# A gated attention and FFN kernel: the high rows of each product follow TensorE's own count, output weights are split in mid-attention, and the last stage has another order

## The chip, the cores and the metric

The kernel runs on one core of one Trainium2 chip. The metric is the device time of one execution in microseconds (us). Three runs of the kernel before gave a median of 1321.56 us (1321.49 to 1323.14). Lower is better.

## The reference

The input x has S = 2048 rows of D = 512. There are H = 32 heads of 16 that share one key and one value head, and an FFN of width F = 1792.

```python
q = (x @ wq).reshape(B, S, H, Dh).transpose(0, 2, 1, 3)
k, v = x @ wk, x @ wv                        # one head for all 32
p = softmax(einsum("bhqd,bkd->bhqk", q, k) * Dh ** -0.5)
a = einsum("bhqk,bkd->bhqd", p, v).transpose(0, 2, 1, 3).reshape(B, S, H * Dh) @ wo
b = (silu(x @ w_gate) * (x @ w_up)) @ w_down
g = sigmoid((x * gate_w).sum(-1, keepdims=True))
out = g * a + (1 - g) * b                    # all f32
```

## The kernel before

**Arithmetic.** Each f32 operand of a large product is split into a rounded high part and the rest (`xh` and `xl`, `wgh` and `wgl`, `hh` and `hl`), and a product is three matmuls: high by high, low by high, high by low. An FFN job of 128 x 512 outputs and 512 inputs so takes 12 matmuls of 128 rows; a job of the down product takes 15 or 12, for 5 or 4 blocks of F.

**Stages.** A prologue transposes x, projects keys and values (`project_kv`) and queries (`query`); in it DVE splits the key and value weights (`prepare_kv`, eight instructions, L111 and L112) between two splits of transposed x (L645 on ACT, L646 on DVE). Then comes attention with the FFN fed into it: a first part of 16 iterations, and 90 blocks of 5, 5 and 6 units (`block`, L838). A unit is one head by 128 keys: two scores (`score`, L774, into the two banks `pss`), two exponentials (ACT L785, some halves after a copy by DVE L780), and four `mix` matmuls (L801, into the bank `po`). Strings in `STEPS` and `TURN` set the order in a block, where S is a score pair and F a step of the FFN; all the block's mix matmuls follow. The block after the first part (block 0) uses `TURN[5]`, with 16 F to 10 S. At the end of a head its output is divided by the sums and stored to `o_d` in DRAM (the items in `LATER`, L812 to L817).

**F steps.** `Halves.step` (L475) cuts a job in its input rows 0 to 63 (the low lane) and 64 to 127 (the high lane), and issues one 64-row matmul for each lane that has a job; the two run side by side in the array. A job runs all its low rows, waits, and then runs its high rows into the same of three banks `pf`. The high rows may start `LAG` = 8 ticks of a step counter after the low rows end, and a bank is taken as free `SLACK` = 8 ticks after the high rows end. For the dependence between lanes, DVE writes one element (`sign`, L498) after the last low matmul, and the first high matmul waits for DVE. A lane without a job leaves its half of the step empty (`idle`). One job, number 54, has only its low rows here (`SPLIT`): its high rows were made earlier (`early`).

**Last stage.** Jobs still in `JOBS` run as 128-row matmuls (`whole`). Ahead of them SP issues loads of the last down weights (`td`, 8), then the four blocks of `wo` (`load_wo`, L142), which go through the two buffers `wraw` and are split by POOL (L152, L154), then the stores of the last head's output (L817) and the read of it (`load_o`, L527, split by POOL in L529 and L532). Then `finish` (L534) multiplies by `wo` for the four chunks of 512 rows in the order `OUTS` = 2, 3, 1, 0, adds the FFN's part and stores. The reads for the second chunk of `OUTS` are issued after all left-over jobs, those of the third and fourth after `finish` of the first and second. `acc_again` and `store_acc` (L418, L426) bring parts of the FFN's sums back and away; one core issues all these transfers on SP in the order of the program.

Of the kernel before, what the change touches and what calls it, by code (L numbers as in the profile page):

```python
# [21 lines left out]
H = 32  # L22
# [44 lines left out]
def tile_gated_mix(ctx, tc, x, wq, wk, wv, wo, w_gate, w_up, w_down, gate_w, out):  # L67
# [13 lines left out]
    x_d = dpool.tile([2, 2, P, KD, CH], F32, name="x_d")  # L81
    w_d = dpool.tile([3, NF, 2, P, D], F32, name="w_d")
    wq_v = wq.rearrange("(k p) n -> p k n", p=P)

# [7 lines left out]
    kmax = cpool.tile([P, 1], F32, name="kmax")  # L92
    sign = cpool.tile([1, 1], F32, name="sign")
    top = cpool.tile([P, KD * NCH + 1], F32, name="top")
# [44 lines left out]
    def load_split(view, name, bufs, pool=wp, order=lambda w, heads=True: w):  # L139
        shape = list(view.shape)  # L140
        raw = wp.tile(shape, F32, name="wraw", bufs=WRB)
        nc.sync.dma_start(raw, view)  # L142
        hi = pool.tile(shape, F32R, name=name + "h", bufs=bufs)
        lo = pool.tile(shape, F32R, name=name + "l", bufs=bufs)
        if pool is qpool:
            split(order(hi, False), order(lo, False), order(raw), nc.gpsimd, nc.gpsimd)
            return hi, lo
        parts = KD if pool is wp else 2
        views = [w if len(shape) == 2 else w.rearrange("p k f -> p (k f)") for w in (hi, lo, raw)]
        cuts = [slice(i * D // parts, (i + 1) * D // parts) for i in range(parts)]  # L150
        for w in cuts if pool is wp else [slice(None)]:
# [39 lines left out]
    class Job:  # L191
        def __init__(self, size, ready, terms, end):
            self.size, self.ready, self.terms, self.end, self.after = size, ready, terms, end, []
            self.only = None


        def step(self, i, half=None):
            alone = half is not None and half == self.only
            opens, closes = alone or not half, alone or half != 0
            if i == 0 and opens:  # L200
                self.ps = ps_f.tile([P, CH], F32, name="pf")
                self.terms = self.terms()
# [5 lines left out]
            ins = nc.tensor.matmul(self.ps, a, b, start=(i == 0 and opens), stop=(last and closes))  # L208
# [86 lines left out]
    def gate_up(n, c):  # L295
# [42 lines left out]
        def up(ps):  # L338
            hh = wp.tile([P, CH], F32R, name="hh", bufs=7)
            hl = wp.tile([P, CH], F32R, name="hl", bufs=7)  # L340
            if len(t) > 2:
# [7 lines left out]
            def cast():  # L349
                if n < NCH * NF - 1:  # L350
# [12 lines left out]
        if n == SPLIT:  # L363
            r[0].only = 0
        return r

# [61 lines left out]
    def jobs():  # L428
        late = []
        for m, c in enumerate(ORDER):  # L430
            for fs in GROUPS:
# [4 lines left out]
                if fs[-1] == NF - 1:  # L436
                    if m < 2:
                        new[-1].after.append(lambda m=m: load_x_again(ORDER[m + 2]))
                    elif m == NCH - 1:
                        new[-1].after.append(acc_again)  # L440
# [6 lines left out]
            late[-1].after.append(lambda c=c: store_acc(c))  # L447
        yield from late
# [19 lines left out]
    class Halves:  # L468
# [6 lines left out]
        def step(self, more):  # L475
# [14 lines left out]
            if self.low:  # L490
# [5 lines left out]
                elif not self.low:  # L496
                    self.wait.append((job, self.clock))
                    tick = nc.vector.memset(sign, 0.0)  # L498
                    follow(tick, job.lows)
                    job.lows = tick  # L500
            if self.high:
# [14 lines left out]
    def load_wo(k, pool):  # L516
        WO.append(load_split(wo[k * P:(k + 1) * P, :], f"wo{k}", 1, pool))

    def load_o(c, ks=range(KD), pool=None):
        if c not in OT:  # L520
            OT[c] = new_x(("o", c))
        for k in ks:
            if pool is None:
                raw = wp.tile([P, CH], F32, name="wraw", bufs=WRB)
            else:
                raw = pool.tile([P, CH], F32R, name="td", bufs=8).bitcast(F32)
            nc.sync.dma_start(raw, o_d[k * P:(k + 1) * P, c * CH:(c + 1) * CH])  # L527
            if c == OUTS[0]:
# [56 lines left out]
    with tc.tile_pool(name="apool", bufs=1) as ap, tc.tile_pool(name="apool2", bufs=2) as a2:  # L585
# [19 lines left out]
        def prepare_kv():  # L605
            k, v, g = slice(0, DH), slice(DH, 2 * DH), slice(2 * DH, 2 * DH + 1)
            for r in (0, RT):
                to = [w[:, :, r:r + 3 * DH].rearrange("p k (i n) -> p k i n", i=3) for w in (wkv_h, wkv_l)]
                src = wkv_f[:, :, k].unsqueeze(2).to_broadcast([P, KD, 3, DH])
                split(to[0], to[1], src, nc.vector)  # L610
            for to, src in ((3 * DH, v), (KW - 1, g)):
                rows = slice(to, to + src.stop - src.start)
                split(wkv_h[:, :, rows], wkv_l[:, :, rows], wkv_f[:, :, src], nc.vector)

# [74 lines left out]
        with tc.manual_schedule():  # L689
# [47 lines left out]
    with tc.tile_pool(name="bpool", bufs=2) as bp:  # L737
        PT = {}

        def load_head(h):  # L740
            nc.sync.dma_start(new_qs(h).bitcast(F32), q_d[h])


        SLOT, HOME, PAST, USED, OLD = {}, {}, {}, {}, {}
# [157 lines left out]
        with tc.manual_schedule():  # L902
# [25 lines left out]
            for k, (u, n) in enumerate(SPANS):  # L928
# [10 lines left out]
                if u % NT == 0 and 0 < h < H - 1:  # L939
                    load_head(h + 1)  # L940
                if k == NB - EARLY:
                    load_o(OUTS[0], range(KD - 1))
            while halves.busy():
# [6 lines left out]
    with tc.tile_pool(name="tpool", bufs=2) as tp, tc.tile_pool(name="rpool", bufs=1, side="right") as rp, \  # L950
            tc.manual_schedule():
        for f in GROUPS[-1]:
            W["d", NCH * NF - NF + f] = [tp.tile([P, D], F32R, name="td", bufs=8) for _ in range(2)]
            for j, part in enumerate(W["d", NCH * NF - NF + f]):
                nc.sync.dma_start(part.bitcast(F32), w_d[2, f, j])
        for k in range(KD):
            load_wo(k, tp)
# [12 lines left out]
        nc.sync.dma_start(ACC[0], a_d[0])  # L970
        for m, c in enumerate(OUTS):
            finish(c, tp)
            if m == 1:

# [6 lines left out]
            if m + 2 < NCH:  # L981
                load_o(OUTS[m + 2], pool=tp)

# [80 lines left out]
```

## Time and profile before

| | |
|---|---|
| median of 3 runs | 1321.56 us (1321.49 to 1323.14) |
| the profiled execution | 1323.07 us; its span in the trace is 1321.3 us, so 1.8 us lie around it |
| busy share of the span | PE 99%, ACT 81%, DVE 59%, POOL 23% |
| clock granted to TensorE | 1.00 of full speed |
| attention blocks 0 to 89 | 129.09 to 1248.24 us |
| left-over jobs in the last stage | 1248.17 to 1271.72 us |
| `finish`, to the last result | 1271.72 to 1321.3 us |

A row of the profile gives start and duration in us, the engine, the line of the program, the operation, the operands by name, and in brackets the idle time before it and what ended that. Two matmuls of 64 rows that start within 0.03 us of each other are the two lanes of one F step.

### The profile page before, as it was taken

The numbers are of one execution on the slowest core, as the hardware profiler recorded it, in microseconds if no ns is written. First come the engines' busy times: TensorE is split into PE (matmuls) and PEld (weight loads), VectorE is DVE, ScalarE is ACT, GpSimd is POOL, SyncE is SP. The second block draws the span as 40 slices with busy tenths as digits, with TensorE's granted clock in tenths as the row PEclk, the third lists the DMA queues.
The fourth block names the chain that finished last, engine by engine and source line by source line (L and its number), as shares of the span: only waits on it lengthen the run. The fifth ranks groups of instructions, "written<-read, shape, count | busy, mean of one in ns | idle before, by whom it ended". The sixth has DMA issues, their size and how long they took to land.

```text
span 1321.3 us, 27265 instructions
## 1 busy us (share of the span) xinstructions
PE 1312.7 (99%) x10767; PEld 769.3 (58%) x10767; DVE 781.7 (59%) x1340; ACT 1075.7 (81%) x1597; POOL 298.6 (23%) x737
## 2 busy tenths in 40 slices
PE   9999999999999999999999999999999999999998
PEld 7655555555555555555555655555655555655587
DVE  4655566566566666666656666666656566566632
ACT  4587888888888888888889888888889888889611
POOL 5362342264053174254120000000000000010043
PEclk9999999999999999999999999999999999999999
DMA  8668121122134264244135252242132252142264
GB/s 287 203 195 278 28 66 37 59 70 61 44 94 164 95 222 148 91 154 160 38 131 180 83 178 69 69 128 89 40 116 95 82 181 85 53 137 88 88 231 146
DMA packets 102516, 157.36 MB, mean 119 GB/s; under 512 B 11888, under 2 KB 43376, under 8 KB 100720
## 3 DMA queue, kind: packets, MB, share of 16 engines
q1 hardware_dynamic: 100656, 155.36, 36.4%
q8 instruction: 88, 1.44, 0.5%
q10 hardware_dynamic: 1728, 0.20, 0.1%
q14 instruction: 44, 0.36, 0.1%
HBM read 99.42 MB, written 55.57 MB: 117 GB/s over the span
## 4 chain that ended last, share of the span: by engine, by line
PE 98%; ACT 1%; DMA 0%; DVE 0%; POOL 0%; SPq 0%; issue 0%; ACTq 0%; POOLq 0%
PE pf L208 39%; PE po L801 34%; PE pss L774 20%; PE pf L121 3%; PE pss L641 0%; ACT pt L785 0%; DMA td<-o_d 0%; PE po L628 0%; POOL xl L532 0%; DVE xl L646 0%; PE pss L681 0%; DVE wkv_l L112 0%; ACT xh L645 0%; SPq L527 0%; DVE wkv_h L111 0%
## 5 line engine op out<-in xcount | busy, mean ns | idle before, releaser
L785 ACT ACTIVATE pt<-pss 128x1024 f32<-128x1024 f32 (+1 forms) x1024 | 787.4, 827 | 156.0 <-PE pss L774 123.2
L780 DVE COPY pt<-pss 128x512 f32<-128x512 f32 x475 | 327.9, 691 | 372.2 <-PE pss L774 367.6
L801 PE MATMUL po<-pt,vaug 128*32 128x512 f32 x4096 | 461.4, 595 | 0.0
L774 PE MATMUL pss<-qs,ks 64*128 64x512 f32 x2048 | 417.7, 410 | 0.4 <-ACT pt L785 0.4
L774 PEld LDWEIGHTS pss<-qs,ks 64*128 64x128 f32 x2048 | 200.1, 183 | 201.8 <-ACT pt L785 102.3
L801 PEld LDWEIGHTS po<-pt,vaug 128*32 128x32 f32 x4096 | 124.8, 109 | 267.2 <-issue 261.9
L785 ACT ACTIVATE pt<-pt 128x512 f32<-128x512 f32 x475 | 265.9, 630 | 0.0
L208 PE MATMUL pf<-xh,wgh 64*128 64x512 f32 (+1 forms) x444 | 160.5, 392 | 0.0
L208 PE MATMUL pf<-xl,wgh 64*128 64x512 f32 (+1 forms) x444 | 159.4, 390 | 0.0
L208 PE MATMUL pf<-xh,wgl 64*128 64x512 f32 (+1 forms) x444 | 159.3, 391 | 0.0
L208 PE MATMUL pf<-xh,wuh 64*128 64x512 f32 (+1 forms) x440 | 154.6, 391 | 0.1
L208 PE MATMUL pf<-xh,wul 64*128 64x512 f32 (+1 forms) x440 | 153.8, 391 | 0.0
L208 PE MATMUL pf<-xl,wuh 64*128 64x512 f32 (+1 forms) x440 | 153.6, 390 | 0.0
L208 PE MATMUL pf<-wdl,hh 64*128 64x512 f32 (+1 forms) x411 | 135.8, 391 | 0.0
L208 PE MATMUL pf<-wdh,hl 64*128 64x512 f32 (+1 forms) x411 | 135.6, 391 | 0.0
L208 PE MATMUL pf<-wdh,hh 64*128 64x512 f32 (+1 forms) x411 | 135.6, 391 | 0.0
L812 DVE RECIPROCAL rsb<-rsb 128x128 f32<-128x128 f32 x128 | 116.6, 933 | 2.0 <-issue 0.4
L529 POOL CAST xh<-wraw 128x512 fp32r<-128x512 f32 x4 | 2.4, 611 | 487.5 <-DMA wraw<-o_d 487.5
L208 PEld LDWEIGHTS pf<-xh,wgh 64*128 64x128 f32 (+1 forms) x444 | 76.6, 185 | 6.7 <-issue 0.6
L208 PEld LDWEIGHTS pf<-xh,wgl 64*128 64x128 f32 (+1 forms) x444 | 76.8, 185 | 5.6
L208 PEld LDWEIGHTS pf<-xl,wgh 64*128 64x128 f32 (+1 forms) x444 | 76.9, 185 | 5.2
L208 PEld LDWEIGHTS pf<-xh,wuh 64*128 64x128 f32 (+1 forms) x440 | 74.3, 185 | 7.2 <-issue 0.7
(171 smaller groups left out, 1447.2 us busy)
## 6 DMA issues: line engine op xcount, KB each, us to landing
qs<-q_d SPq DMA_DIRECT2D x31, 512.0 KB, 4.5
q_d<-hh SPq DMA_DIRECT2D x28, 256.0 KB, 4.1
wraw<-in_B_w_gate_dram SPq DMA_DIRECT2D x28, 256.0 KB, 4.0
wraw<-in_B_w_up_dram SPq DMA_DIRECT2D x28, 256.0 KB, 3.1
wraw<-in_B_w_down_dram SPq DMA_DIRECT2D x28, 256.0 KB, 3.5
wgh<-w_d SPq DMA_DIRECT2D x28, 256.0 KB, 2.7
wgl<-w_d SPq DMA_DIRECT2D x28, 256.0 KB, 3.0
wuh<-w_d SPq DMA_DIRECT2D x28, 256.0 KB, 2.7
```

The lines of the kernel that those rows point to most:

```text
L121: nc.tensor.matmul(ps, a, b, start=(i == 0), stop=(i == n - 1))
L208: ins = nc.tensor.matmul(self.ps, a, b, start=(i == 0 and opens), stop=(last and closes))
L529: nc.gpsimd.tensor_copy(OT[c][0][:, k, :], raw)
L774: nc.tensor.matmul(ps[:, b * CH:(b + 1) * CH], ks[rows, kt * P:(kt + 1) * P], QS[h][rows, j, :], start=True, stop=True)
L780: other = nc.vector.tensor_copy(pt[:, CH:], ps[:, CH:])
L785: ins = nc.scalar.activation(pt[:, w], ps[:, w], AF.Exp, scale=SCALE)
L801: ins = nc.tensor.matmul(po[c * 2 * DH:(c + 1) * 2 * DH, :], vaug[:, kt, :], pt[:, c * CH:(c + 1) * CH], start=(kt == 0), stop=(kt == NT - 1))
L812: nc.vector.reciprocal(rsb[:, w], rsb[:, w])
```

## The change

- `LAG` goes from 8 to 3 and `SLACK` from 8 to 9. The DVE instruction `sign` is gone: a TensorE `nop` after the last low matmul carries the dependence, and in the built program the first high matmul waits for TensorE's own count.
- Block 0 has its own string with 20 F to 10 S, and DVE copies three of its ten score halves.
- In the last group of FFN jobs, all gates and ups come before the late downs. Up 54 may run only once gate 54 has its bank. Results of jobs 54 and 55 lie in the tiles `wgh`, `wgl`; the high part of 54 is made by ACT, that of 55 by DVE.
- `wo` is loaded and split in mid-attention (`keep_wo`, with gate 39, 41, 43 and 45), its parts are stored to a new DRAM buffer `o_w`, and the last stage only loads the parts.
- Two of the four pairs of last down weights are loaded before the end of attention (`load_last`).
- `load_o` is divided: `fetch_o` issues the reads, `split_o` makes the parts. The reads for the second chunk come before the left-over jobs, those for the third and fourth before `finish` of the first and second. `acc_again` and the read of `again` move behind the first `finish`, the last `store_acc` behind the third.
- `prepare_kv` goes from DVE to POOL, ahead of the split of the first query weights.

```diff
-SLACK = 8
+SLACK = 9
-LAG = 8
+LAG = 3
...
+    def keep_wo(k):
+        lo, hi = [wp.tile([P, D], F32R, name="wraw", bufs=WRB) for _ in range(2)]
+        nc.sync.dma_start(lo.bitcast(F32), wo[k * P:(k + 1) * P, :])
+        for i in range(KD):
+            w = slice(i * P, (i + 1) * P)
+            nc.gpsimd.tensor_copy(hi[:, w], lo[:, w].bitcast(F32))
+            nc.gpsimd.tensor_tensor(lo[:, w], lo[:, w].bitcast(F32), hi[:, w].bitcast(F32), ALU.subtract)
+        KEPT.extend([lambda j=j, part=part: nc.sync.dma_start(o_w[k, j], part.bitcast(F32))
+                     for j, part in enumerate((hi, lo))])
...
+            if nm == "g" and n % 2 and n // 2 - NF - 5 in range(KD):
+                keep_wo(n // 2 - NF - 5)
...
             if half is not None:
                 rows = slice(half * RT, (half + 1) * RT)
                 a, b = a[rows], b[rows]
+                if half and i == 0 and not alone:
+                    follow(nc.tensor.nop(), self.lows)
             ins = nc.tensor.matmul(self.ps, a, b, start=(i == 0 and opens), stop=(last and closes))
             if half == 0:
                 self.lows = ins
-            elif half and i == 0 and not alone:
-                follow(ins, self.lows)
...
+            r[1].ready = lambda: ("u", n) in W and r[0].bank is not None
...
                 for j, job in enumerate(new):
                     yield job
-                    if late and j:
+                    if late and j and ns[-1] < NCH * NF - 1:
                         yield late.pop(0)
...
                     self.wait.append((job, self.clock))
-                    tick = nc.vector.memset(sign, 0.0)
-                    follow(tick, job.lows)
-                    job.lows = tick
...
-                split(to[0], to[1], src, nc.vector)
+                split(to[0], to[1], src, nc.gpsimd, nc.gpsimd)
...
+            prepare_kv()
             load_wq(0)
             transpose_x(0, 0)
-            prepare_kv()
...
-                    block(k, u, n, u + 1, end, TURN[n], "A" * m, [f"{i}d" for i in range(m)])
+                    block(k, u, n, u + 1, end, "FFFSFFSFFSFFSFFSFFSFFSFFSFFFSS", "AAAHAHAHAA", "0d 1d 2d 3d 4d 5d 6d 7d 3s 5s 7s | 8d 9d".split())
...
-        for k in range(KD):
+        for k in range(2):
             load_wo(k, tp)
...
         while LATER:
             LATER.pop(0)[1]()
-        load_o(OUTS[0], [KD - 1])
+        for k in range(2, KD):
+            load_wo(k, tp)
+        fetch_o(OUTS[0], [KD - 1])
+        fetch_o(OUTS[1], pool=tp)
+        assert JOBS[0].ready()
+        whole(JOBS.pop(0))
+        split_o(OUTS[0], [KD - 1])
+        split_o(OUTS[1])
         while JOBS:
             assert JOBS[0].ready()
-
             whole(JOBS.pop(0))
-        load_o(OUTS[1], pool=tp)
-        nc.sync.dma_start(ACC[0], a_d[0])
         for m, c in enumerate(OUTS):
+            if m + 2 < NCH:
+                fetch_o(OUTS[m + 2], pool=tp)
+            if m == 1:
+                acc_again()
+                nc.sync.dma_start(ACC[0], a_d[0])
             finish(c, tp)
+            if m == 2:
+                store_acc(ORDER[-1])
...
             if m + 2 < NCH:
-                load_o(OUTS[m + 2], pool=tp)
+                split_o(OUTS[m + 2])
```

**Where instructions now stand.** The built programs have these counts. Of the matmuls of jobs, 4132 stand before the last mix in the program before and 4182 in the program after; behind the last mix stand 101 matmuls of jobs before (two of them half-row) and 75 after. Block 0 has 4 more F steps; no other block has a different number. Of the counter's 2054 steps before, 58 half places are empty (45 of them in mid-attention); of 2056 after, 14 are (3 in mid-attention).

On PE in a block, before: a job's first high matmul (the first row with `DVE_49`) waits for DVE's count, and an order's row gives the full shape for a half-row matmul too.

```order
L208 MATMUL pf<-xh,wul 128x512
L208 MATMUL pf<-xl,wgh 128x512
L208 MATMUL pf<-xh,wuh 128x512
L774 MATMUL pss<-qs,ks 128x512 [waits Activation_49]
L774 MATMUL pss<-qs,ks 128x512
L208 MATMUL pf<-xh,wgl 128x512 [waits Pool_49]
L208 MATMUL pf<-xl,wuh 128x512
L208 MATMUL pf<-xh,wul 128x512
L208 MATMUL pf<-xh,wuh 128x512 [waits DVE_49,Pool_49]
```

The same engine after, in a like place:

```order
L799 MATMUL pss<-qs,ks 128x512 [waits DVE_49,Activation_49]
L799 MATMUL pss<-qs,ks 128x512
L221 MATMUL pf<-xh,wgh 128x512 [waits Pool_49]
L221 MATMUL pf<-xl,wuh 128x512
L221 MATMUL pf<-xl,wgh 128x512
L221 MATMUL pf<-xh,wul 128x512
L221 MATMUL pf<-xh,wgl 128x512 [waits Pool_49]
L221 MATMUL pf<-wdh,hh 128x512 [waits PE_49]
```

The wait is on the matmul itself and is for PE's own count. In the program after, the nearest such start stands 8 half-row matmuls (4 steps) behind the last low one that it waits for, and most stand 19 to 25 behind.

On SP at the start of the last stage, before: the third and fourth raw load of `wo` wait for POOL, and the last head's stores and the read of them stand behind.

```order
L142 DMA wraw<-in_A_wo_dram 128x512 [waits DMAHW5_49,DMAHW3_49,Pool_49]
L142 DMA wraw<-in_A_wo_dram 128x512 [waits DMAHW6_49,DMAHW4_49,Pool_49]
L817 DMA o_d<-osb 16x512 [waits DMAHW7_49,DVE_49]
L817 DMA o_d<-osb 16x512 [waits DMAHW0_49]
L817 DMA o_d<-osb 16x512 [waits DMAHW1_49]
L817 DMA o_d<-osb 16x512 [waits DMAHW2_49]
L527 DMA wraw<-o_d 128x512 [waits DMAHW5_49,DMAHW1_49,Pool_49]
```

After, two blocks of ready parts stand ahead of the stores and two behind; the reads of the last head's rows and of the second chunk (`td`) follow at once:

```order
L529 DMA wo1l<-o_w 128x512 [waits DMAHW2_49]
L842 DMA o_d<-osb 16x512 [waits DMAHW3_49,DVE_49]
L842 DMA o_d<-osb 16x512 [waits DMAHW4_49]
L842 DMA o_d<-osb 16x512 [waits DMAHW5_49]
L842 DMA o_d<-osb 16x512 [waits DMAHW6_49]
L529 DMA wo2h<-o_w 128x512 [waits DMAHW7_49]
L529 DMA wo2l<-o_w 128x512 [waits DMAHW0_49]
L529 DMA wo3h<-o_w 128x512 [waits DMAHW1_49]
L529 DMA wo3l<-o_w 128x512 [waits DMAHW2_49]
L539 DMA wraw<-o_d 128x512 [waits DMAHW5_49,DMAHW3_49,Pool_49]
L539 DMA td<-o_d 128x512 [waits DMAHW4_49]
```

None of these waits for POOL's splits of `wo` any more; the one wait for POOL is for the buffer of `wraw`.

On DVE in the prologue, before (`xl` is the split of transposed x; ahead of these rows stand the first `xl` and one more pair of 48 columns):

```order
L111 CAST wkv_h<-wkv_f 128x4x48
L112 TENSOR_TENSOR wkv_l<-wkv_f,wkv_h 128x4x48
L111 CAST wkv_h<-wkv_f 128x4x16
L112 TENSOR_TENSOR wkv_l<-wkv_f,wkv_h 128x4x16
L111 CAST wkv_h<-wkv_f 128x4
L112 TENSOR_TENSOR wkv_l<-wkv_f,wkv_h 128x4
L646 TENSOR_TENSOR xl<-pss,xh 128x4x256
```

After, the two `xl` follow each other:

```order
L710 MEMSET warm 128x64
L664 TENSOR_TENSOR xl<-pss,xh 128x4x256 x2
L636 TENSOR_REDUCE sel<-ident 128x8
L637 COPY spread<-ident 16x128
L638 MEMSET vaug 128x16x16
```

The eight instructions of `wkv` now stand on POOL, between the making of `ident` and the split of `wq0`.

More of the change, by code (lines that the diff above doesn't have):

```diff
@@ L82, in tile_gated_mix @@
     w_d = dpool.tile([3, NF, 2, P, D], F32, name="w_d")
+    o_w = dpool.tile([KD, 2, P, D], F32, name="o_w")
     wq_v = wq.rearrange("(k p) n -> p k n", p=P)
@@ L147, in load_split @@
             return hi, lo
-        parts = KD if pool is wp else 2
         views = [w if len(shape) == 2 else w.rearrange("p k f -> p (k f)") for w in (hi, lo, raw)]
-        cuts = [slice(i * D // parts, (i + 1) * D // parts) for i in range(parts)]
-        for w in cuts if pool is wp else [slice(None)]:
+        cuts = [slice(i * P, (i + 1) * P) for i in range(KD)]
+        for w in cuts:
             nc.gpsimd.tensor_copy(views[0][:, w], views[2][:, w])
@@ L193, in __init__ @@
             self.size, self.ready, self.terms, self.end, self.after = size, ready, terms, end, []
-            self.only = None
+            self.only, self.bank = None, None
         def step(self, i, half=None):
@@ L338, in up @@
         def up(ps):
-            hh = wp.tile([P, CH], F32R, name="hh", bufs=7)
-            hl = wp.tile([P, CH], F32R, name="hl", bufs=7)
+            if n < NCH * NF - 2:
+                hh, hl = [wp.tile([P, CH], F32R, name="h" + x, bufs=7) for x in "hl"]
+            else:
+                hh, hl = [wp.tile([P, KD, P], F32R, name="wg" + x, bufs=2).rearrange("p k f -> p (k f)") for x in "hl"]
             if len(t) > 2:
@@ L446, in jobs @@
                 late = [down(ns, c, i) for i in range(TC)]
-            late[-1].after.append(lambda c=c: store_acc(c))
+            if m < NCH - 1:
+                late[-1].after.append(lambda c=c: store_acc(c))
         yield from late
@@ L516, in load_wo, with fetch_o, split_o @@
     def load_wo(k, pool):
-        WO.append(load_split(wo[k * P:(k + 1) * P, :], f"wo{k}", 1, pool))
-    def load_o(c, ks=range(KD), pool=None):
+        WO.append([pool.tile([P, D], F32R, name=f"wo{k}{x}", bufs=1) for x in "hl"])
+        for j, part in enumerate(WO[-1]):
+            nc.sync.dma_start(part.bitcast(F32), o_w[k, j])
+    RAW = {}
+    def fetch_o(c, ks=range(KD), pool=None):
+        for k in ks:
+            if pool is None:
+                RAW[c, k] = wp.tile([P, CH], F32, name="wraw", bufs=WRB)
+            else:
+                RAW[c, k] = pool.tile([P, CH], F32R, name="td", bufs=8).bitcast(F32)
+            nc.sync.dma_start(RAW[c, k], o_d[k * P:(k + 1) * P, c * CH:(c + 1) * CH])
+    def split_o(c, ks=range(KD)):
         if c not in OT:
@@ L522, in load_o @@
         for k in ks:
[L523 to L527, printed above, removed]
+            raw = RAW.pop((c, k))
             if c == OUTS[0]:
@@ L609, in prepare_kv @@
                 src = wkv_f[:, :, k].unsqueeze(2).to_broadcast([P, KD, 3, DH])
-                split(to[0], to[1], src, nc.vector)
+                split(to[0], to[1], src, nc.gpsimd, nc.gpsimd)
             for to, src in ((3 * DH, v), (KW - 1, g)):
                 rows = slice(to, to + src.stop - src.start)
-                split(wkv_h[:, :, rows], wkv_l[:, :, rows], wkv_f[:, :, src], nc.vector)
+                split(wkv_h[:, :, rows], wkv_l[:, :, rows], wkv_f[:, :, src], nc.gpsimd, nc.gpsimd)
         spread = ap.tile([DH, DH, HG], F32, name="spread")
@@ L741, in load_head, with load_last @@
             nc.sync.dma_start(new_qs(h).bitcast(F32), q_d[h])
+        def load_last(i):
+            f = GROUPS[-1][i]
+            td = qsp.tile([P, 2, CH], F32R, name="qs")
+            W["d", NCH * NF - NF + f] = [td[:, j] for j in range(2)]
+            for j in range(2):
+                nc.sync.dma_start(td[:, j].bitcast(F32), w_d[2, f, j])
         SLOT, HOME, PAST, USED, OLD = {}, {}, {}, {}, {}
@@ L938, in tile_gated_mix @@
                 h = u // NT
-                if u % NT == 0 and 0 < h < H - 1:
-                    load_head(h + 1)
+                if u % NT == 0 and h:
+                    load_head(h + 1) if h < H - 1 else load_last(0)
                 if k == NB - EARLY:
-                    load_o(OUTS[0], range(KD - 1))
+                    fetch_o(OUTS[0], range(KD - 1))
+                    split_o(OUTS[0], range(KD - 1))
+            load_last(1)
             while halves.busy():
```

11 lines of the change are left out of this document (4 added, 7 removed).

## The prediction

> **What bounds the kernel.** I read the page first, then what PE waits for, the chain of work that ended last, the busy time by stage, and the timeline at the places that the change touches.
>
> ```profile
> span 1321.3 us, 27265 instructions
> PE 1312.7 (99%) x10767; PEld 769.3 (58%) x10767; DVE 781.7 (59%) x1340; ACT 1075.7 (81%) x1597; POOL 298.6 (23%) x737
> ...
> PE 98%; ACT 1%; DMA 0%; DVE 0%; POOL 0%; SPq 0%; issue 0%; ACTq 0%; POOLq 0%
> ```
>
> PE is the bound nearly everywhere: it holds 98% of the chain. So time can come only from fewer PE steps or from PE's few waits.
>
> By stage (first PE's busy time, then PEld, DVE, ACT, POOL):
>
> ```profile
> 129.09:137.09 8.00, 7.63 (x53) 3.85 (x53) 4.09 (x9) 8.00 (x9) 5.35 (x16) 1.00 0.29 98
> 137.09:1242.95 1105.86, 1105.79 (x9441) 626.00 (x9445) 676.95 (x1165) 973.91 (x1473) 211.23 (x590) 1.00 0.31 100
> ```
>
> Block 0 alone has ACT busy through all its 8.00 us; the other 89 blocks have PE busy through all of theirs at a granted clock of 1.00. In the chain, the mix matmuls mark the blocks (start, us, what):
>
> ```profile
> 137.09 4.43 PE po L801 x40
> 1106.80 4.43 PE po L801 x40
> 1118.41 4.43 PE po L801 x40
> 1131.45 5.29 PE po L801 x48
> 1143.92 4.43 PE po L801 x40
> ...
> 1248.24 23.65 PE pf L208 x101
> ```
>
> Three undisturbed blocks last 11.61, 13.04 and 12.48 us, 37.13 together. The 89 periods that begin at 137.09 are 29 such threes and two more (11.61 and 13.04): 1101.4 of the 1105.86 us, so some 4.5 us are lost in small stalls.
>
> **The change, part by part.** All is worked against the profiled execution: 1323.07 us, 1.51 above the median of the runs, so the result is lowered by 1.51 at the end.
>
> *Left-over jobs.* Behind the last mix stand 101 matmuls before and 75 after.
>
> ```profile
> 1248.17 0.49 PE L208 MATMUL pf<-wdl,hh 64*128 64x512 f32 x1
> ...
> 1248.82 0.50 PE L208 MATMUL pf<-wdh,hh 128*128 128x512 f32 x1
> ...
> 1271.72 0.39 PE L121 MATMUL pf<-wo0h,xh 128*128 128x512 f32 x1
> ...
> 1284.88 0.40 PE L121 MATMUL pf<-wo3l,xh 128*128 128x512 f32 x1
> 1285.47 0.50 PE L121 MATMUL pf<-wo3h,xl 128*128 128x512 f32 x1 [0.19 <-POOL xl L532]
> 1285.81 0.39 PE L121 MATMUL pf<-wo0h,xh 128*128 128x512 f32 x1
> ```
>
> From 1271.72 to 1284.88 are 58 steps, 0.227 us each. The stage took 1271.72 - 1248.17 = 23.55 us. After: 75 x 0.227 = 17.0, and some 0.4 for a slow start (the first two here took 0.65 instead of 0.45) and a short wait for `hl` of the last gate and up: 17.45. Gain 6.1.
>
> For these 26 matmuls nothing is paid in attention, if an empty half place costs as much as a full one. The step counts say that the same F steps now hold 50 more half-row matmuls, and the trace prices an empty place:
>
> ```profile
> 1240.92 0.39 PE L208 MATMUL pf<-wdh,hh 64*128 64x512 f32 x1
> 1241.15 0.39 PE L208 MATMUL pf<-wdl,hh 64*128 64x512 f32 x1
> ```
>
> A single lane steps every 0.23 us; two lanes step in 0.24 (358.16 to 358.40 in the rows of the denser lanes, below). At most 0.01 for each of 48 places, 0.5, is paid; I take the gain as the whole 6.1.
>
> *The wait on PE's own count* (and no DVE instruction). DVE's 160 writes of 59 ns are cheap and DVE has room. What matters is how late PE sees its own end:
>
> ```profile
> 1226.49 0.39 PE L208 MATMUL pf<-xh,wul 64*128 64x512 f32 x1
> 1226.94 0.06 DVE L498 MEMSET sign<- 1x1 f32 x1 [0.53 <-PE pf L208]
> ```
>
> The last low matmul starts at 1226.49 and DVE sees its end 0.45 us later. The nearest high start in the built order stands 4 steps behind, about 0.93 us, so the count has come 0.48 before it is asked for; most stand further. While PE waits, all stands behind it, score and mix too, so a stall would be paid in full. Bounds: 0 for each wait (above), to 0.25 (a step that met a late release, next rows). I take 0, the nearest row.
>
> *Denser lanes.* A bank is now reused sooner after its last high matmul's evacuation, by DVE or ACT.
>
> ```profile
> 357.99 0.74 DVE L412 SCALAR_TENSOR_TENSOR acc<-pf,c_sb,acc 128x512 f32<-128x512 f32 x1
> ...
> 358.16 0.39 PE L208 MATMUL pf<-xl,wgh 64*128 64x512 f32 x1
> ...
> 358.40 0.39 PE L208 MATMUL pf<-xh,wgl 64*128 64x512 f32 x1
> 358.88 0.47 PE L208 MATMUL pf<-xh,wuh 64*128 64x512 f32 x1
> ```
>
> DVE left the bank at 358.73 and the next job's first low matmul came at 358.88 instead of 358.63: 0.25 lost. The 4.5 us over the blocks' own lengths are some 18 of these. Taking `sign` out shortens DVE's queue, `SLACK` gives a tick more, but the reuse is denser; from -3 (half of them gone) to +3 us. I take -0.5, as the tick more acts on each of them and the density on the 45 former gaps alone.
>
> *Block 0.* Its scores wait for ACT (start and releaser):
>
> ```profile
> 128.55 0.73 PE L774 MATMUL pss<-qs,ks 64*128 64x512 f32 x4
> 136.59 0.50 PE L774 MATMUL pss<-qs,ks 64*128 64x512 f32 x2 [0.18 <-ACT pt L785]
> ```
>
> From 128.55 to the mix at 137.09 are 8.54 us for 10 S and 16 F. PE's 26 steps need only 26 x 0.23 = 6.0 of them. The new string has 30 steps (20 F), the number of the undisturbed blocks whose steps last 11.61 - 4.43 = 7.18; and DVE copies three halves, which frees their banks sooner and lets ACT finish the last exponentials beside the mix. So the block gains between 0 (ACT holds it as before) and 1.36 (down to 7.18), and takes 4 more steps for nothing, which are part of the 50 matmuls above. ACT's ten exponentials all remain, so I take a value nearer to the first: -0.5.
>
> *Prologue.*
>
> ```profile
> 8.86 1.03 ACT L645 ACTIVATE xh<-pss 128x1024 fp32r<-128x1024 f32 x1 [1.12 <-PE pss L641]
> ...
> 10.68 1.22 DVE L646 TENSOR_TENSOR xl<-pss,xh 128x1024 fp32r<-128x1024 f32 x1
> ...
> 11.95 1.09 PE L641 MATMUL pss<-ident,xt 128*128 128x128 f32 x8 [1.28 <-DVE xl L646]
> ```
>
> The second `xl` needs `xh`, done at 9.89, and started at 10.68 behind the eight `wkv` instructions. Now it starts at 9.91: -0.77, all of it in PE's wait of 1.28. The cover is that POOL is done with `wkv` before `project_kv` at about 12.0:
>
> ```profile
> 1.79 0.53 ACTq L598 DMA_DIRECT2D wkv_f<-in_gate_w_dram  x1
> ...
> wkv_f<-in_gate_w_dram ACTq DMA_DIRECT2D x1, 2.0 KB, 6.5
> L111 POOL CAST wgh<-hh 128x512 fp32r<-128x512 f32 x1 | 0.6, 602 | 0.0
> L112 POOL TENSOR_TENSOR wgl<-hh,wgh 128x512 fp32r<-128x512 f32 x1 | 1.3, 1295 | 0.1
> ```
>
> The last of the three small loads (issue, then KB and us to landing) is there at 1.79 + 6.5 = 8.3. The four pairs of POOL have 192, 192, 64 and 4 columns, 452 in all, less than the 512 of the pair in the other rows (1.9 us). Even if all loads came as late as the last, POOL would end by 10.2 and the starts of eight instructions, with 1.8 us for these up to 12.0. Without that cover the 0.77 would be gone and more. Bounds: -0.77 and 0; I take -0.77, since the reserve is more than the rows need. The split of `wq0`, now behind it on POOL, has `project_kv` and a chunk's transposes ahead of its use.
>
> *The reads for the second chunk of `finish`.* In the rows of the first fence the steps 1284.88 to 1285.81 took 0.93 instead of 0.45, waiting for POOL's `xl`. These reads now come before the left-over jobs, some 10 us earlier: -0.47.
>
> *The rest lies beside other work.* `keep_wo` gives POOL 32 instructions in mid-attention (POOL is busy 211 of 1106 us there) and SP 4 loads and 8 stores of 256 KB at a DMA share of 0.31. Its 8 loads in the last stage replace 4 loads, and 4 pairs of weights come early. The `store_acc` at the end has `finish` of a whole chunk ahead of the last output. Cover for the last head's rows:
>
> ```profile
> 1254.51 0.69 DVE L815 TENSOR_TENSOR osb<-osb,rsb 128x512 f32<-128x512 f32 x1
> ...
> 1263.04 1.77 SPq L817 DMA_DIRECT2D o_d<-osb  x4
> ...
> 1268.02 0.36 SPq L527 DMA_DIRECT2D wraw<-o_d  x1
> ...
> 1271.92 1.29 POOL L532 TENSOR_TENSOR xl<-wraw,xh 128x512 fp32r<-128x512 f32 x1
> ```
>
> From the first store to POOL's end took 10.2 us (1263.04 to 1273.21). The quotient was done at 1255.20, 7.0 us after the last mix; now one evacuation of the FFN (0.74) and the wait ahead of it no longer stand before it on DVE, which puts it at about 5.8. Its stores follow, so `xl` is ready at 16.0; the last k of the first tile needs it at 19.5 (17.45 and 9 steps). Cover: 3.5 us.
>
> The Trainium skill, page "SBUF — State Buffer", section "SBUF: two separate sides", says that a DVE instruction with two SBUF inputs and a GpSimd instruction that reads SBUF exclude each other for their whole length. That speaks against moving splits to POOL's mid-attention time: by it some 8 `hl` of DVE could each wait out one subtraction of POOL (128 of the 512 columns of the 1.3 us above, 0.33), an estimate of 2.6 us on DVE. The rows of `hl` by stage say less (count, busy, mean ns):
>
> ```profile
> L354 DVE TENSOR_TENSOR hl<-ht,hh 128x512 fp32r<-128x512 f32 x11 | 8.0, 730 | 0.4
> L354 DVE TENSOR_TENSOR hl<-ht,hh 128x512 fp32r<-128x512 f32 x13 | 9.0, 692 | 0.4
> ```
>
> The first is from 430 to 660 us, where POOL splits weights, the second from 700 to 950, where it rests: 38 ns each, 0.3 us in all, and DVE is not on the path. By either the sum stays.
>
> **Sum.** -6.1 - 0.5 - 0.5 - 0.77 - 0.47 = -8.3: the profiled execution comes to 1314.8 and the median to 1313.2.
>
> **The rivals.**
>
> *The last head's rows come late.* If its stores waited as long behind the quotient as before (18.0 us from 1255.20 to 1273.21), `xl` would be ready at 23.8, not at 19.5: PE waits 4.3 us, a time of 1317.5. For it: SP still has loads ahead of the stores. Against: none of these waits for POOL now.
>
> *The denser lanes stall.* One of about 7 job changes (150 in all) more that meets an unfinished evacuation is 20 x 0.25 = +5: about 1318.2. For it: 18 such stalls exist already. Against: DVE is 61% busy there.
>
> *Filling a place isn't free.* If a filled place cost 0.12 us more than an empty one, 48 would cost 5.8 and 1319.0 would be left, no change that can be told. Against: the rows of a single lane above.
>
> *PE drains at each wait on its own count* (the other side). If the wait holds back the queue until PE is empty, each of 160 costs up to the 0.25 of the late release, +40: 1353. From 8.3/160 = 0.052 us each it is slower than 1321.56. For it: no row of before shows PE waiting for itself in attention. Against: the 0.45 us above lies within the 4 steps.
>
> **How the numbers follow.** The forecast has 0.68: with the bounds of block 0 and the stalls it lies within 1309.5 and 1316.5. The last head late has 0.10 (1317.5), the stalls 0.12 (1318), the dear places 0.05 (1319), draining 0.05 (1353). A measurement of this kernel tells about 0.2% (2.6 us) from no change. Faster: 0.68 + 0.10 + 0.12 = 0.90; same 0.05; slower 0.05. The range from 1308.5 to 1318 holds the forecast and the two rivals next to it but for their outer parts, 0.8.
>
> **What will show it.** Right: from the last mix to `finish` about 17.5 us and 75 matmuls; the first mix of block 0 to the last 0 to 3 us less than 1105.86; PE's wait in the prologue 0.5; no wait for POOL in `finish`; PE waits for itself nowhere. Wrong: a row of PE waiting on PE at L221, a last stage in which `finish` stands still at its tenth step, blocks longer than 11.61, 13.04 and 12.48, or the `wkv` rows of POOL ending after 12.

## The result and the profile after

The changed kernel takes 1313.54 us (median of 4 runs, 1312.90 to 1314.03) against 1321.80 of the kernel before beside it: a ratio of 0.9936 (95% interval 0.9922 to 0.9949). The forecast was 1313.2. The profiled execution took 1313.23 us. Its page begins and ends its chain like this:

```profile
span 1311.4 us, 27136 instructions
PE 1304.0 (99%) x10791; PEld 764.8 (58%) x10791; DVE 779.2 (59%) x1175; ACT 1075.2 (82%) x1600; POOL 305.7 (23%) x765
...
PE 99%; DMA 1%; SPq 0%; DVE 0%; issue 0%
```

The list of what PE waits for (us in total, times, longest) is now this, in full. Nothing in attention or in the last stage is on it. PE's weight loads (PEld) have a list of their own, and no row of it waits for PE:

```profile
PE pss L659 <- DMA xt<-in_A_x_dram: 1.0, 3, 0.5
PE po L646 <- DVE warm L710: 1.0, 1, 1.0
PE pss L659 <- DVE xl L664: 0.5, 1, 0.5
```

By stage (us of the stretch, then busy us of PE, PEld, DVE, ACT, POOL): block 0 before and after, and the 89 blocks behind it, to be read against the 1105.86 of before (the last mix starts at 1238.54, so they are 1102.84 to the hundredth).

```profile
128.62:137.09 8.47, 8.10 (x56) 4.27 (x59) 4.56 (x9) 8.00 (x9) 5.35 (x16) 1.00 0.34 112
127.36:135.70 8.34, 8.32 (x64) 5.23 (x68) 5.35 (x9) 6.92 (x10) 5.58 (x16) 1.00 0.34 112
135.70:1238.50 1102.80, 1102.80 (x9483) 625.63 (x9483) 679.75 (x1025) 975.22 (x1476) 224.18 (x622) 1.00 0.32 104
```

The end of the chain (start, us, what) after:

```profile
1238.54 5.52 PE po L826 x48
1244.06 17.32 PE pf L221 x75
1261.38 22.40 PE pf L121 x96
...
1283.90 22.65 PE pf L121 x108
```

Before, the first two rows had 5.29, and 23.65 for 101 matmuls; the row of the last two chunks was this:

```profile
1294.28 22.15 PE pf L121 x108
```

And PE's first steps of the left-over jobs and of `finish`:

```profile
1243.99 0.50 PE L221 MATMUL pf<-xh,wuh 128*128 128x512 f32 x1
...
1261.22 0.39 PE L121 MATMUL pf<-wo0h,xh 128*128 128x512 f32 x1
...
1272.18 0.40 PE L121 MATMUL pf<-wo3h,xl 128*128 128x512 f32 x1
```

So the 9.9 us between the two spans are, from front to back (less time is a gain): 1.26 ahead of block 0 (128.62 to 127.36), 0.12 in block 0, 3.0 in the blocks, 6.1 from the start of the last mix to `finish` (1242.95 to 1271.72 was 28.77, 1238.54 to 1261.22 is 22.68), and 0.6 lost again in `finish` (to the last matmul 44.71 before, 45.33 now). From 1261.22 to 1272.18 are 47 steps: 0.233 us each, where 0.227 were expected. This loss has nothing to do with a wait.

### The profile page after: what moved, and what is told of

Its sections match the earlier page's. It is cut to its first block, busy times and chain, and to the rows that moved or that the text cites. A ratio compares the mean times of both kernels' runs of the same rounds, so it can differ in the third digit from the quotient of the medians.

```text
span 1311.4 us, 27136 instructions
## 1 busy us (share of the span) xinstructions
PE 1304.0 (99%) x10791; PEld 764.8 (58%) x10791; DVE 779.2 (59%) x1175; ACT 1075.2 (82%) x1600; POOL 305.7 (23%) x765
## 4 chain that ended last, share of the span: by engine, by line
PE 99%; DMA 1%; SPq 0%; DVE 0%; issue 0%
PE pf L221 39%; PE po L826 35%; PE pss L799 20%; PE pf L121 4%; DMA xt<-in_A_x_dram 1%; PE pss L659 0%; PE pss L699 0%; SPq L610 0%; DVE ot L565 0%; PE po L646 0%; PE po L693 0%; PE po L1012 0%
## 5 line engine op out<-in xcount | busy, mean ns | idle before, releaser
L799 PE MATMUL pss<-qs,ks 64*128 64x512 f32 x2048 | 410.5, 406 | 0.0
L221 PE MATMUL pf<-xh,wgh 64*128 64x512 f32 x448 | 162.4, 392 | 0.0
L221 PE MATMUL pf<-xl,wgh 64*128 64x512 f32 x448 | 162.4, 391 | 0.0
L221 PE MATMUL pf<-xh,wgl 64*128 64x512 f32 x448 | 160.7, 391 | 0.0
L221 PE MATMUL pf<-wdh,hh 64*128 64x512 f32 (+1 forms) x411 | 142.9, 390 | 0.0
L221 PE MATMUL pf<-wdl,hh 64*128 64x512 f32 (+1 forms) x411 | 142.9, 390 | 0.0
L221 PEld LDWEIGHTS pf<-xl,wgh 64*128 64x128 f32 x448 | 77.4, 184 | 6.2 <-issue 0.8
L221 PEld LDWEIGHTS pf<-xh,wgh 64*128 64x128 f32 x448 | 77.5, 185 | 5.8
L221 PEld LDWEIGHTS pf<-xh,wgl 64*128 64x128 f32 x448 | 77.4, 185 | 5.5
L221 PEld LDWEIGHTS pf<-xl,wuh 64*128 64x128 f32 (+1 forms) x444 | 76.1, 185 | 5.5
```

The costliest lines, as they stand in the source:

```text
L799: nc.tensor.matmul(ps[:, b * CH:(b + 1) * CH], ks[rows, kt * P:(kt + 1) * P], QS[h][rows, j, :], start=True, stop=True)
```

## The experiments

All are of one core; ratios are to the kernel before beside them, with their 95% intervals.

**The lane part undone** in the changed kernel:

```diff
-SLACK = 9
-LAG = 3
+SLACK = 8
+LAG = 8
...
+                    tick = nc.vector.memset(sign, 0.0)
+                    follow(tick, job.lows)
+                    job.lows = tick
```

> The changed kernel with the lane part undone: LAG 8, SLACK 8 and the write of `sign` by DVE as the tick, no wait of TensorE on its own count; `sign` is allocated, so addresses are those of the left shift. Its built program has 97 left-over matmuls (75 with the lane part) and 4145 before the last mix (4182). Theory of the prediction (the denser lanes are the gain, a filled place is free): 22 x 0.227 = 5.0 us more than the left shift, 1317.2 us if that is at 1312.2. Rival (a filled place costs 0.12 us): less than 3 us more. If the wait on TensorE's own count costs something, the blocks here are shorter than 11.62, 13.04 and 12.48 us.

1322.23 us, 0.9999 (0.9990 to 1.0009): not 1317.2. The last stage is as expected (chain, below): from the last mix's end to the end of the span 71.35 us against 66.27 with the left shift (the changed kernel with these addresses, under Addresses below), 5.08 for 22 matmuls, 0.231 each. But the 89 blocks take 1107.0 us, 4.6 more than with the left shift (1102.38). Some 3.0 of that are small stalls: about 20 blocks are over 0.1 us longer than 11.61, 13.04 and 12.48, as in the kernel before, where the changed kernel has 8. And one block alone loses 1.6, since weights came late (first row; the other two are the end of the chain):

```profile
992.54 0.50 PE L220 MATMUL pf<-wdh,hh 64*128 64x512 f32 x1 [0.93 <-DMA wdh<-w_d]
...
1243.26 5.29 PE po L830 x48
1248.55 22.45 PE pf L220 x97
```

So without the lanes all the other parts bring nothing that can be told. That one of them delayed these weights (`keep_wo` has its loads and stores on the same queue) is likely and was not run by itself; the changed kernel has no such wait.

**The lane part alone** in the kernel before:

```diff
-SLACK = 8
-LAG = 8
+SLACK = 9
+LAG = 3
...
+                if half and i == 0 and not alone:
+                    follow(nc.tensor.nop(), self.lows)
...
-                    tick = nc.vector.memset(sign, 0.0)
```

> The kernel before with the lane part alone: LAG 3, SLACK 9, no write of `sign` by DVE (the tile stays allocated, so the addresses are those of before), the wait on TensorE's own count. Its built program has 83 left-over matmuls instead of 101 and 24 empty half places instead of 58. Theory (the lane part carries the change): 18 x 0.227 = 4.1 us less in the last stage and 3 us less of stalls in the blocks, 1314.9 us. Rival (the gain needs the other parts, block 0, the order of jobs, the early weights): no more than 3 us less, 1319 us or above.

1318.16 us, 0.9968 (0.9956 to 0.9980), between the two. The blocks take 1104.45 us (137.14 to 1241.59) instead of 1105.86. All but the last together have 2.9 us less of stalls. The last can't be compared by this, since ten of its 48 mix matmuls and one step of a left-over job now stand ahead of 1241.59:

```profile
1239.32 1.83 PE po L798 x10
1241.15 0.43 PE pf L210
1241.59 4.42 PE po L798 x38
```

The last stage gained less than its 18 matmuls, for two waits that are new there, and one that has stayed:

```profile
PE pf L210 <- ACT hh L353: 0.8, 1, 0.8
PE pf L210 <- DVE hl L354: 0.5, 1, 0.5
...
PE pf L121 <- POOL xl L529: 0.3, 1, 0.3
```

With fewer jobs left over, the result of the last gate and up is needed before it is ready. The other parts mend this: the changed kernel has none of the three waits. So lanes alone give 4.0 and the rest alone 0. Both together give 9.3 with tiles at the same addresses (the left shift below, 1322.01 to 1312.70; the changed kernel as it stands gives 8.3 to 8.6). Some 5.3 us thus come only from both at once. The late weights (1.6) and the two waits (1.3) are part of that; the rest of it was not taken apart.

**The order of the last jobs undone** in the changed kernel (with it the place of `hh`, `hl` of 54 and 55, the engine of their casts, and the condition of up 54):

```diff
-                    if late and j and ns[-1] < NCH * NF - 1:
+                    if late and j:
...
-                if n != SPLIT:
+                if n < NCH * NF - 1:
```

> The changed kernel with the order of the last FFN jobs undone: late downs come between the last gates and ups again, up 54 needn't wait for gate 54's bank, results of 54 and 55 lie in `hh` and `hl`, and ACT makes the high part of 55. Its built program has 74 left-over matmuls (75) and 4186 ahead of the last mix (4182), but gate and up 55 now run in the last stage, 9 steps ahead of the matmul that needs their result. Theory (this part pays only together with the lanes: with the lane part alone PE waited 1.3 us for `hh` and `hl` in the last stage): PE waits some 1.3 us for hh and hl, 1315 us. Rival (the downs ahead cover that chain): no such wait, 1313.5 us.

1328.46 us, 1.0049 (1.0036 to 1.0063): the wait is there, but it is 11.7 us, and the kernel is slower than before. The rows (PE's wait; then DVE and ACT in order of time) show why:

```profile
PE pf L221 <- ACT hh L364: 11.7, 1, 11.7
...
1254.14 0.69 DVE L354 TENSOR_TENSOR ht<-ht,pf 128x512 f32<-128x512 f32 x1
...
1261.63 2.49 ACT L546 ACTIVATE xh<-td 128x512 fp32r<-128x512 f32 x4 [8.32 <-DMA td<-o_d]
1264.03 0.61 ACT L364 ACTIVATE hh<-ht 128x512 fp32r<-128x512 f32 x1
```

The `ht` of job 55 was ready at 1254.83, but ACT sat idle for 8.32 us and made `hh` last: it takes its instructions in order. The early `split_o` of the second chunk puts ACT's `xh` behind a read that stands behind the last head's stores on SP, and `hh` stands behind that `xh`. So with the early reads the new order of jobs and the cast's move to DVE are needed; which of these two does it was not run apart.

**The reads at their old places** in the changed kernel:

```diff
-        fetch_o(OUTS[1], pool=tp)
         assert JOBS[0].ready()
         whole(JOBS.pop(0))
         split_o(OUTS[0], [KD - 1])
-        split_o(OUTS[1])
...
+        fetch_o(OUTS[1], pool=tp)
+        split_o(OUTS[1])
         for m, c in enumerate(OUTS):
-            if m + 2 < NCH:
-                fetch_o(OUTS[m + 2], pool=tp)
...
+                fetch_o(OUTS[m + 2], pool=tp)
                 split_o(OUTS[m + 2])
```

> The changed kernel with the reads of the attention output back where they were: those of the second chunk after all left-over jobs, those of the third and fourth after finish of the first and second. Theory of the prediction (the early reads take away PE's wait for POOL's xl in finish, 0.47 us): that wait comes back, 0.5 to 1 us, 1314.0 to 1314.5. Rival (the reads are hidden either way now that the last stage loads wo ready): no wait in finish and 1313.5.

1313.54 us, 0.9935 (0.9921 to 0.9948): the rival holds. PE's waits, in full:

```profile
PE po L646 <- DVE warm L710: 1.0, 1, 1.0
PE pss L659 <- DMA xt<-in_A_x_dram: 0.6, 2, 0.5
PE pss L659 <- DVE xl L664: 0.5, 1, 0.5
```

So it wasn't the earlier reads that took the wait of before away. It stays with the lane part alone (0.3) and is gone with all the other parts and no lanes, so one of these took it. The likeliest are the splits of `wo`, which POOL no longer has there; that part was not run by itself.

**Each wait on PE's own count put right behind the matmul that it waits for:**

```diff
-                    follow(nc.tensor.nop(), self.lows)
+                    follow(nc.tensor.nop(), LATEST[0])
             ins = nc.tensor.matmul(self.ps, a, b, start=(i == 0 and opens), stop=(last and closes))
+            LATEST[:] = [ins]
```

> The changed kernel, but the first high matmul of a job waits for the matmul issued just before it (the low lane of the same step) and not for the last low one of its own job, which ended long before. Same order of instructions. This prices the wait itself. Theory of the prediction (a wait costs what is missing until the end is seen, 0.45 us after the start): some 160 waits of 0.4 us, 1313.5 + 64 = 1378 us. Rival (the wait drains PE whenever it stands there, so that the changed kernel pays already): less than 20 us more, since most is paid in the changed kernel too.

1397.62 us, 1.0570 (1.0555 to 1.0584), 84.1 more than the changed kernel beside it (1313.52). The profile shows it at the weight loads of the first high matmuls, not in PE's own list (us in total, times, longest):

```profile
PEld pf L223 <- PE pf L223: 79.5, 162, 0.5
```

So 162 waits cost 0.52 us each (84.1 / 162). The changed kernel has the same instructions in the same order, with the awaited matmul four steps or more back, and no such row at all: its waits are free, and what makes them so is the distance alone.

**A tick less of lag, one more of slack** (`LAG` 2, `SLACK` 10, and the shift of the right side described next):

> The changed kernel with the 32 bytes on the right side, LAG 2 and SLACK 10: the same 75 left-over matmuls and 14 empty half places, a bank is taken as free one tick later and the high rows may start one tick earlier. Theory (the stalls left in the blocks, 1.5 us over the undisturbed lengths, are first low matmuls that meet an unfinished evacuation): some of them go, 0.3 to 1 us less than the right shift alone, which was at 1312.5 where the changed kernel was at 1313.5. Rival (the wait on TensorE's own count, now at three steps, 0.7 us, begins to cost): PE waits for PE appear at the step line, and the time is 1313.5 or more.

1312.31 us, 0.9925 (0.9912 to 0.9939), against 1313.52 of the changed kernel beside it on the same chip; the ranges don't touch (1312.00 to 1312.77, 1313.24 to 1313.99). But the blocks take 1102.99 us, 0.35 more than with the shift alone: the stalls that remain did not go, and PE doesn't wait for PE. This theory fell; the gain is that of the shift, as its chain has 21.76 us for the first two chunks of `finish` too.

**The changed kernel once more**, as the partner of the last two and of the lane part alone:

> The changed kernel as it is, beside the next three on the same chip. Both theories: 1313.5 us within 0.5, ratio 0.9936.

1313.52 us, 0.9934 (0.9921 to 0.9948).

**Addresses.** The slow steps of `finish` have the same operands, shapes and granted clock (1.00) as before. What differs is the place of the tiles: without `sign` (4 bytes, 32 with its padding) every tile allocated behind it on the left side of the buffer lies 32 bytes lower; tiles of the right side (x, the split attention output) stay. Five kernels move one side or the other, with no other difference:

```diff
+    sign = cpool.tile([1, 1], F32, name="sign")          # left side, 32 bytes
...
+    ypool = tc.alloc_tile_pool(name="ypool", bufs=1, side="right")
+    ypool.tile([1, 1], F32, name="pad")                  # right side, 32 bytes
...
+    pad0 = cpool.tile([1, 1], F32, name="pad0")          # two: 64 bytes; three: 96
```

> The changed kernel with one thing put back: the tile `sign` (4 bytes, 32 of the buffer) stays allocated, but nothing writes it, so all tiles of the left side lie 32 bytes further on, as in the kernel before. Theory 1 (addresses): a 128-row matmul steps in 0.233 us when its moving and its stationary tile lie at different offsets modulo 64 bytes, and in 0.227 when they agree; with `sign` gone the weights of wo lie at 0 and the split attention output at 32, so `finish` (192 steps) and up 54 (12) each lose 0.0067 us a step. Expected here: 0.2267 us a step in finish, finish about 1.3 us shorter, 1312.2 us in all, and up to some us less if the steps of two lanes in attention pay too. Theory 2 (the last stage's transfers or its other order slow the steps): 0.2333 stays, 1313.5 us within 0.5.

> The changed kernel with 32 bytes allocated on the right side instead, so that the tiles of x, of the split attention output and half of the `pt` tiles move to offset 0 modulo 64 and agree with everything else (scores and mix as well). Theory 1 (addresses): finish at 0.2267 us a step as with the left shift, so about 1312.2 us; if scores and mix pay for a mismatch too, less than the left shift's time, where qs lies at 32 and ks at 0. Theory 2 (transfers or order): 0.2333 a step and 1313.5 us.

> The kernel before with 32 more bytes allocated and unused on the left side, so that its weights lie at offset 0 modulo 64 and x at 32, as in the changed kernel. Theory 1 (addresses): finish at 0.2333 us a step instead of 0.2267 and the same for the left-over gate 55 and up jobs (36 steps): 228 x 0.0067 = 1.5 us, 1323.3 us, more if attention's steps pay. Theory 2: no change, 1321.8 us within 0.5.

> The changed kernel with 64 unused bytes more on the left side. All left tiles move, but their offset modulo 64 stays 0 against 32 on the right (modulo 128: wo at 0, the split attention output at 96). If the rule is agreement modulo 64: finish stays at 0.2333 us a step, 1313.5 us. If any other place of the left tiles would do (the changed kernel's was unlucky in some other way): 0.2267 a step and 1312.3 to 1312.7.

> The changed kernel with 96 unused bytes more on the left side: wo at 32 and the split output at 96 modulo 128, so they agree modulo 64 (32 and 32) and not modulo 128. If the rule is agreement modulo 64: finish at 0.2267 us a step, 1312.3 to 1312.7 us. If it is modulo 128 or more: 0.2333 and 1313.5.

The chain's rows of `finish` (96 matmuls of the first two chunks, 108 of the others, 24 of these of 256 columns), in this order: 32 bytes left, 32 right, 32 bytes more in the kernel before, 64 left, 96 left:

```profile
1260.30 21.76 PE pf L122 x96
...
1282.18 22.15 PE pf L122 x108
```

```profile
1260.93 21.76 PE pf L123 x96
...
1282.81 22.15 PE pf L123 x108
```

```profile
1272.13 22.39 PE pf L122 x96
...
1294.65 22.61 PE pf L122 x108
```

```profile
1262.39 22.39 PE pf L123 x96
...
1284.90 22.61 PE pf L123 x108
```

```profile
1261.93 21.97 PE pf L124 x96
...
1284.03 22.29 PE pf L124 x108
```

| kernel | place of `wo`, of the split output, modulo 128 bytes | us a step | time, ratio |
|---|---|---|---|
| before | 96, 96 | 0.2267 | |
| before, 32 more | 0, 96 | 0.2333 | 1323.31, 1.0013 (1.0004 to 1.0022) |
| changed | 64, 96 | 0.2333 | 1313.54, 0.9936 |
| 32 left | 96, 96 | 0.2267 | 1312.70, 0.9929 (0.9915 to 0.9942) |
| 32 right | 64, 64 | 0.2267 | 1312.51, 0.9927 (0.9913 to 0.9940) |
| 64 left | 0, 96 | 0.2333 | 1313.29, 0.9932 (0.9917 to 0.9947) |
| 96 left | 32, 96 | 0.2289 | 1312.93, 0.9931 (0.9916 to 0.9946) |

(Steps are worked out as 22.40 / 96 and the like; for the kernel before, from the 58 steps in the prediction. The places are those of the built programs.) The address, not the transfers or the order, sets the step: the same program gains or loses 0.007 us a step by 32 bytes. The rule as expected, agreement modulo 64, is only nearly right: with 64 bytes between them the step lies between the two. In the trace the difference shows in steps of full 128 rows alone. The blocks of attention, where two lanes of 64 rows run, take 1102.84, 1102.38 and 1102.64 us in the changed kernel, with 32 left and with 32 right: at 0.007 a step they would differ by several us. Why is not shown here. The intervals of these ratios overlap; for the time as a whole the pair on one chip above (1312.31 against 1313.52) is the better evidence, though that kernel has the other `LAG` and `SLACK` as well.

## Why the prediction was right, point by point

The time and the forecast differ by 0.3 us, but two terms of the sum were wrong by more, on opposite sides.

- *Left-over jobs, -6.1.* Right. From the first left-over matmul to `finish` it is 1261.22 - 1243.99 = 17.2 us (17.45 expected) against 23.55. A filled place costs nothing: 22 more left over cost 5.08 in the last stage when the lanes were undone, while the blocks, into which 50 more matmuls went, became shorter.
- *The wait on PE's own count, 0.* Right, for the reason given. The upper bound was too low: not 0.25 but 0.52 us is at stake each time.
- *Denser lanes, -0.5.* The direction was right and the size wrong: -3.0, the end of the range, and two thirds of the 4.5 us, not half. The step that failed was to weigh the 45 former gaps against the added tick: the blocks became denser and lost less. Undoing the lane part brings the stalls back (1107.0), the lane part alone takes 2.9 us of them away. So they go with that part as a whole; which of `LAG`, `SLACK` and the end of `sign` does it was not run apart. Nor does the trace of before show some 18 meetings with an unfinished evacuation, 0.25 us each: only the one step in the prediction's rows starts that late. No other F step of these blocks is more than 0.11 us late, so the stalls are many and small, and what most of them wait for stays open.
- *Block 0, -0.5.* It was -0.12, with 4 more steps, which are counted with the left-over jobs. ACT is busy 6.92 of the 8.34 us now, but the block is still 1.16 longer than the 7.18 of an undisturbed one, and weight loads of scores still wait for ACT, half as much as before (us in total, times, longest; before, then after):

```profile
PEld pss L774 <- ACT pt L785: 4.4, 9, 0.8
PEld pss L799 <- ACT pt L810: 2.1, 6, 0.5
```

  So the value nearer to "ACT holds it" was the right side to take, and still too large.
- *Prologue, -0.77.* Right for the wait: 1.28 became 0.51. POOL's cover was ample, done at 7.72 for a need at 11.15:

```profile
7.51 0.21 POOL L112 TENSOR_TENSOR wkv_l<-wkv_f,wkv_h 128x4 fp32r<-128x4 f32 x1
...
9.02 1.23 DVE L664 TENSOR_TENSOR xl<-pss,xh 128x1024 fp32r<-128x1024 f32 x1 [1.03 <-ACT xh L663]
...
10.30 1.09 PE L659 MATMUL pss<-ident,xt 128*128 128x128 f32 x8 [0.51 <-DVE xl L664]
```

  The other 0.5 of the 1.26 ahead of block 0 goes with when x lands, which differs from execution to execution: the transposes ahead of this wait began at 9.61 before and at 8.73 after, and a later part of x then made PE wait 0.27.
- *Early reads, -0.47.* The wait went, but not because of the early reads, as the late reads show: that the term came out is luck. And `finish` became 0.6 longer, since the step rose from 0.227 to 0.233: 192 x 0.0067 = 1.3, less the wait. The sum had no term for this; it took a matmul's step to be a constant of its shape.
- *The last head's rows.* `xl` was ready 16.4 us after the mix (16.0 expected; T = 1243.99), 3.0 ahead of need:

```profile
1259.04 1.30 POOL L550 TENSOR_TENSOR xl<-wraw,xh 128x512 fp32r<-128x512 f32 x1
```

- *POOL's splits beside DVE.* `hl` takes 692 ns in the stretch in which `wo` is split, as without, but in this trace none of them ran beside one of the 32 splits, so this says nothing on their price. Once a DVE instruction with two inputs in the buffer was first, and POOL paid (0.80 us for a cast of 0.29):

```profile
994.56 0.69 DVE L344 SCALAR_TENSOR_TENSOR ht<-ht,hs 128x512 f32<-128x512 f32 x1 [0.36 <-ACT ht L336]
...
994.61 0.80 POOL L164 CAST wraw<-wraw 128x128 fp32r<-128x128 f32 x1 [22.58 <-DMA wraw<-in_A_wo_dram]
```

  By the rule of the Trainium skill, "SBUF — State Buffer", section "SBUF: two separate sides", whichever starts first holds the shared ports and the other blocks; the trace agrees here, with 0.5 us on POOL, where nobody waits for it. The other way round `hl` took 0.83 us at 388.10, beside a subtraction of POOL that had begun at 387.74.

One sum of the prediction is off, though nothing hangs on it: with the bounds of block 0 and the stalls the forecast lies within 1309.8 and 1317.2, not 1309.5 and 1316.5.

By the spans the terms sum to -9.9, not -8.3. The medians differ by 8.3 because the profiled execution of before stood 1.3 us above its median and that of after 0.3 below. Which execution is profiled so moves a sum of this kind by about 1.5 us. The agreement to 0.3 is in part luck: the stalls gave 2.5 us more than forecast, `finish` 1.1 less, and the two profiled executions stood where they stood.

## What to carry to other kernels

A wait of TensorE on its own count cost 0.52 us here at no distance and nothing at four steps: put the distance of a few steps between, and take the other engine out of the handshake. Parts of a change that share a queue hang together: an early read that an engine converts puts all its later work behind that read. And where removing a small tile moves others, compare the matmuls' step before and after; giving 32 bytes back, on either side, won here about 1 us, and the version with them on the right, `LAG` 2 and `SLACK` 10, at 1312.31 us, is faster than both kernels.

## What the runs showed of the hardware that was not expected

- The step of a 128-row f32r matmul of 512 columns is 0.227, 0.229 or 0.233 us by the relative place of its two operands modulo 128 bytes (0 apart; 64 apart, in one kernel; 32 or 96 apart), at a granted clock of 1.00.
- The same difference wasn't seen where two 64-row matmuls run side by side (blocks of 1102.38 to 1102.84 us).
- A wait for the matmul issued just before costs 0.52 us, more than the 0.45 from its start to another engine's reaction.
